# Five small edits to a fused attention and MLP kernel: sums, corner matmuls, staging, cosine, and which engine splits

## The chip, the cores and the metric

One core of one Trainium2 chip runs the whole program. The metric is the device time of one execution in microseconds (us). The engines of the core are named as in the profile: PE (TensorE matmuls), PEld (TensorE weight loads), DVE (VectorE), ACT (ScalarE), POOL (GpSimd), and SP, which here only issues DMAs.

## The reference, cut to what matters

The program is an attention with a learned bias, followed by two MLP layers. Everything is float32, the weights come as 8-byte floats.

```
scores = q @ k.T / 8 + bias(h, i, j)          # 4 batches x 8 heads, 576 x 576, head size 64
attn   = exp(scores - max) ; attn = attn / (sum(attn) + 1e-9)
x      = attn @ v                              # -> 2304 tokens x 512
h = x @ w_in1 ; x1  = (h * cos(h)) @ w_out1    # 512 -> 2048 -> 512
h = x1 @ w_in2; out = (max(h,0) + alpha*min(h,0)) @ w_out2
```

bias(h, i, j) is a small MLP of log1p(|i-j|) / log1p(max(i,1)) with 32 hidden values.

## The kernel before, in words

**Precision by splitting.** A float32 operand is cut into a rounded high part (`hi`) and the rest (`lo = x - hi`), and each product is three matmuls: hi*hi, hi*lo, lo*hi. The high part is a copy to a rounded type, the low part a subtraction. Five places do this: `split_qk` for q and k (high part of q on ACT in L312, of k on DVE in L314, both low parts on POOL in L319), `weight` for weights (L183 to L188), `split_x` for the MLP's inputs (L594 on DVE, L596 on DVE and POOL in turns), `split_g` for the activations (L641 on ACT, L642 on POOL).

**Bias.** 36 groups (`bias_phase`) of DVE, PE and ACT work write the bias matrix to memory; they fill the first 90 us or so and are interleaved with the first attention stages.

**Attention.** 16 pairs (two heads of one batch), each in two units: A (row blocks 0 and 1) and B (row blocks 2 and 3 and the remaining 64 rows of both heads, stage 0). The first four pairs do their A units first. A stage is `emit_S` (scores on PE, in 64-row tiles of the array; one PSUM buffer), `emit_max` (L348, DVE: adds the bias, takes the row maximum) and `emit_exp` (L360, ACT, with row sums). When all stages of a unit are through, `recip` adds 1e-9 to the sums (L368), inverts them (L369) and has POOL spread them over 64 columns (`rb`, L371). Then come the unit's fillers on PE, in the order that ORDER gives: 0 to 3 and R transposes (`T_full`, `T_rem`), v to z products with v (`PV`, L441 and L444), L the last transposes (`T_last`, L426 and L430), N the transposes of the inverse sums (`norm`, L379 and L384). They are put between the scores of the next stages by a credit of 1 us per half stage. In unit B, L and N each end with two matmuls of 64 x 64 corners (L430 and L384; each is four passes in the trace, since float32 takes two passes). L392 and L394 are the copies out of PSUM on ACT and DVE. Transposes take turns on three PSUM banks (`t_bank`).

**Staged weights.** The first eight of the 16 blocks of layer 1's weights are converted during attention and written to memory (`stage_w`, 16 pieces): load, L169 and L170 on ACT, L172 and L173 on DVE, L176 on POOL, high part on ACT (L184), low part on DVE (L188), store (L195). There is one buffer `st`. A new piece is let in at half stage WS0 + WSR * ns; `step` advances one generator by one yield per half stage, of the first two in the list in turns, and the rest runs after the last stage. The other eight blocks of layer 1 are converted directly during the first token tile of the MLP (`direct_w`).

**MLP.** Per layer 5 token tiles (3 of 512, 2 of 384 tokens) times 16 blocks f. `emit_h` (L608, 12 matmuls) fills one of four PSUM banks; `act1` applies h*cos(h): ACT writes h/(2 pi) + 1/4 (L617), DVE rounds it to a whole number by adding and subtracting a large constant (L618), takes that many turns off h in two steps (L619, L620), ACT takes the sine (L622), DVE multiplies by h (L623), which frees the bank; then L641 and L642. `emit_o` (L658, L660, 12 or 9 matmuls) follows four blocks behind; `evac` (L668, L670) empties its banks at the end of a tile.

**Order.** A planner with a model of durations puts the instructions of each engine in order; each engine then runs its list strictly in that order.

Of the kernel before, what the change touches and what calls it, by code (L numbers as in the profile page):

```python
# [19 lines left out]
B, H, S, D = 4, 8, 576, 64  # L20
# [4 lines left out]
NCC = DM // 128  # L25
HS = S // 2
NG = S // 16
MAGIC = 12582912.0
C1 = 6.28125
C2 = 2.0 * math.pi - C1  # L30
TILES = [(0, 512), (512, 512), (1024, 512), (1536, 384), (1920, 384)]
PITCH = S + 32
QC = S + 64
HP, LP, XP, CPRI, SP = 200, 0, 300, -50, 400
HIA = (1, 1, 1, 1)
LOP = (0, 0, 0, 0)
EV_A, EV_M = 5, 6
UPB, EPB = {"D": 11, "A": 4}, 4
PBUF, BTB = 6, 10
FIRST, SIDE, SMOD, BFIRST, BRATE, SPL, WS0, WSR, PER = 4, 6, 2, 16, 1.25, 3, 24, 7.3, 1.0  # L40
XL, XS, OEB, LA = 7, 12, 3, 4
KEEP = (1, 1)
QUOTA0, QUOTA1, NSF = 9, 2, 8
# [1 line left out]

UNIT = {"A": ((0, 1), 0), "B": ((2, 3), 1)}

ORDER = {"A": "012vw3LNxyz", "B": "01R2vw3LNxyz"}
TENG = {"A": "vava-a", "B": "vavava"}


# [6 lines left out]
def attn_mlp_kernel(ctx: ExitStack, tc: tile.TileContext, a: dict, out: bass.AP):  # L58
    nc = tc.nc
    ve, se, ge, te, sy = nc.vector, nc.scalar, nc.gpsimd, nc.tensor, nc.sync  # L60
# [99 lines left out]
    def weight(layer, f, part, hi, lo, hi_act, lo_pool):  # L160
        src = (a["wi1"], a["wi2"])[layer][f] if part == 0 else (a["wo1"], a["wo2"])[layer][f * 128:(f + 1) * 128, :]
        nm = f"{layer}_{f}_{part}"
        if wide:
            raw = wpool["s"].tile([128, 512, 2], I32, tag="raw", name=f"raw{nm}")
            sy.dma_start(out=raw.rearrange("p n t -> p (n t)"), in_=src.bitcast(I32))
            yield
            c = wpool["c"].tile([128, 512], I32, tag="c", name=f"wc{nm}")
            p = wpool["c"].tile([128, 512], I32, tag="p", name=f"wp{nm}")
            se.activation(out=c.bitcast(F32), in_=raw[:, :, 1].bitcast(F32), func=AF.Copy, scale=2.0 ** -112)  # L169
            se.activation(out=p, in_=raw[:, :, 0].bitcast(U32), func=AF.Copy, scale=2.0 ** -29)  # L170
            yield
            ve.tensor_scalar(c, c, 3, None, op0=ALU.logical_shift_left)  # L172
            ve.scalar_tensor_tensor(out=c, in0=raw[:, :, 1], scalar=-2 ** 31, in1=c,  # L173
                                    op0=ALU.bitwise_and, op1=ALU.bitwise_or)
            yield
            ge.tensor_tensor(out=c, in0=c, in1=p, op=ALU.add)  # L176
            yield
            w = c.bitcast(F32)
        else:
            w = wpool["s"].tile([128, 512], F32, tag="raw", name=f"raw{nm}")  # L180
            sy.dma_start(out=w, in_=src)
            yield
        if hi_act:  # L183
            keep(0, se.activation(out=hi, in_=w, func=AF.Copy))  # L184
        else:
            keep(0, ve.tensor_copy(out=hi, in_=w))
        yield
        keep(1, (ge if lo_pool else ve).tensor_tensor(out=lo, in0=w, in1=hi.bitcast(F32), op=ALU.subtract))  # L188
        yield
# [42 lines left out]
    def attention():  # L232
        with ExitStack() as c:
# [26 lines left out]
            Pp = {}  # L260
            Tt = {}
            T5t = {}
            xps = {}
            raws = {}
            sums = {}
            Rt = {}
            place = {(1 + i, h): (u, 2 * x + h) for u, (t, rem) in UNIT.items() for x, i in enumerate(t) for h in range(2)}
            place[0, 0] = ("B", 4)
            count = {"s": 0, "t": 0, "x": 0}

            def turn(which, pools):
                count[which] += 1
# [2 lines left out]
            def t_bank(name):  # L275
                return turn("t", ps_t).tile([128, 512], F32, tag="t", name=name)
# [29 lines left out]

            def split_qk(n):
                t = []
                for r, nm, eng in zip(raws.pop(n), "qk", (se, ve)):
                    hi, lo = (qk_p.tile([128, QC], F32R, tag=nm + x, name=f"{nm}{x}{n}") for x in "hl")  # L310
                    if eng is se:
                        se.activation(out=hi, in_=r, func=AF.Copy)  # L312
                    else:
                        ve.tensor_copy(out=hi, in_=r)  # L314
                    t.append((r, hi, lo))
                yield
                qk[n] = [x for r, hi, lo in t for x in (hi, lo)]
# [38 lines left out]
            def emit_exp(n, s, h, e, nm):  # L356
                u, col = place[s, h]
                if (n, u) not in sums:
                    sums[n, u] = m_p.tile([128, 5], F32, tag="sm", name=f"sm{n}_{u}")
                keep(3, se.activation(out=e, in_=e, func=AF.Exp, bias=nm, scale=-1.0,  # L360
                                      accum_out=sums[n, u][:, col:col + 1]))
                Pt[n, s, h] = e


            def recip(n, u):
                m = 4 + SIZE[u][1]
                sm = sums.pop((n, u))[:, 0:m]
                ve.tensor_scalar(sm, sm, 1e-9, None, op0=ALU.add)  # L368
                ve.reciprocal(out=sm, in_=sm)  # L369
                rb = x_p.tile([128, 5, 64], F32, tag="rb", name=f"rb{n}_{u}")  # L370
                ge.tensor_copy(out=rb[:, 0:m, :], in_=sm.unsqueeze(2).to_broadcast([128, m, 64]))  # L371
                Rt[n, u] = rb

            def norm(n, u):
                t, rem = SIZE[u]
                rb = Rt[n, u]
                ps = t_bank(f"N{n}_{u}")
                for x in range(t):
                    te.transpose(out=ps[:, 128 * x:128 * x + 128],  # L379
                                 in_=rb[:, 2 * x:2 * x + 2, :].rearrange("p a b -> p (a b)"), identity=ident)  # L380
                if rem:
                    for h in range(2):
                        r = slice(64 * h, 64 * h + 64)
                        te.matmul(ps[r, 128 * t:128 * t + 64], lhsT=rb[r, 4, :], rhs=ident[r, r],  # L384
                                  start=True, stop=True)
                R = x_p.tile([128, 320], F32, tag="R", name=f"R{n}_{u}")
                cpy("a", R[:, 0:QW[u]], ps[:, 0:QW[u]])
                Rt[n, u] = R
# [23 lines left out]
            def T_rem(n, u, eng):  # L412
# [4 lines left out]
                                 identity=ident)  # L417
                cpy(eng, Tt[n, u][:, :, :, w:w + 64], ps.rearrange("p (c h q) -> p c h q", c=4, h=2))

            def T_last(n, u, eng):  # L420
                t, rem = SIZE[u]
                T5 = T_p.tile([128, 320], F32, tag="T5", name=f"T5{n}_{u}")
                T5t[n, u] = T5
                ps = t_bank(f"T5{n}_{u}")
                for x, i in enumerate(UNIT[u][0]):
                    te.transpose(out=ps[:, 128 * x:128 * x + 128], in_=Pp[n, i][:, 512:640], identity=ident)  # L426
                if rem:
                    for h in range(2):
                        r = slice(64 * h, 64 * h + 64)
                        te.matmul(ps[r, 128 * t:128 * t + 64], lhsT=Pt[n, 0, 0][r, 512:S], rhs=ident[r, r],  # L430
                                  start=True, stop=True)
                cpy(eng, T5[:, 0:QW[u]], ps[:, 0:QW[u]])

            def PV(n, u, cc):
# [137 lines left out]
    def mlp():  # L572
        with ExitStack() as c:
# [38 lines left out]
            def act1(t, f, ps):  # L612
                n = TILES[t][1]
                h = ps[:, 0:n]
                tt = t_p.tile([128, 512], F32, tag="ta", name=f"ta{t}_{f}")[:, 0:n]
                g = t_p.tile([128, 512], F32, tag="tb", name=f"tb0_{t}_{f}")[:, 0:n]
                se.activation(out=tt, in_=h, func=AF.Identity, scale=1.0 / (2.0 * math.pi), bias=quart)  # L617
                ve.tensor_scalar(tt, tt, MAGIC, MAGIC, op0=ALU.add, op1=ALU.subtract)  # L618
                ve.scalar_tensor_tensor(out=g, in0=tt, scalar=-C1, in1=h, op0=ALU.mult, op1=ALU.add)  # L619
                ve.scalar_tensor_tensor(out=g, in0=tt, scalar=-C2, in1=g, op0=ALU.mult, op1=ALU.add)  # L620
                yield
                se.activation(out=g, in_=g, func=AF.Sin, bias=hpi)  # L622
                ve.tensor_tensor(out=g, in0=h, in1=g, op=ALU.mult)  # L623
                split_g(0, t, f, g)
                yield
# [165 lines left out]
```

## Time and profile before

| | us |
|---|---|
| median of 3 runs | 1198.11 (1197.49 to 1198.72) |
| profiled execution | 1197.57 |
| span of its instructions | 1195.7 |

Busy share of the span: PE 94%, PEld 74%, DVE 63%, ACT 45%, POOL 32%. PE's share is a sum over overlapping, pipelined matmuls; that it is high says that PE seldom stands still, not that its work could not be shorter. The attention fills the first 375 us or so, layer 1 of the MLP runs from there to about 800 us, layer 2 to the end.

### The profile page before, as it was taken

Reading aid. Unit: us, or ns where it says so; the run is one execution under the profiler, and the core shown is the slowest. Engines: PE = TensorE matmul, PEld = TensorE weight load, DVE = VectorE, ACT = ScalarE, POOL = GpSimd, SP = SyncE. Lnnn points to the kernel's source line nnn. Section 1 sums busy time; section 2 is a strip of 40 time slices with the busy share of each in tenths; the row PEclk is TensorE's granted clock in tenths of the full one; section 3 lists DMA queues with packets and bytes.
Section 4 is the critical chain, followed back from the end, with each engine's and each line's share of the span. In section 5 each row is a group of like instructions: output and inputs, shape, how many; then the busy total and the mean of one; then the engine's idle time right before and its main releaser. Section 6 shows DMA issues by size and latency. Waiting matters only on the chain.

```text
span 1195.7 us, 17301 instructions
## 1 busy us (share of the span) xinstructions
PE 1128.2 (94%) x6376; PEld 890.5 (74%) x6376; DVE 758.1 (63%) x1390; ACT 536.5 (45%) x1038; POOL 388.4 (32%) x330
## 2 busy tenths in 40 slices
PE   5688999899999898899999999999999999999998
PEld 1145666566666687688888999998788888899997
DVE  7897677877767899756756757787652242242322
ACT  5786676666763775443444554544411111111111
POOL 4003333333103555323333334354542222222222
PEclk7798999999999899899999999999999999999999
DMA  7764655656214544212112224644220010000000
GB/s 243 225 181 154 193 185 186 225 192 197 87 50 153 198 127 138 71 51 82 71 55 79 104 68 148 224 149 154 88 71 1 15 48 1 25 38 1 27 1 27
DMA packets 56084, 129.47 MB, mean 108 GB/s; under 512 B 8000, under 2 KB 15168, under 8 KB 53952
## 3 DMA queue, kind: packets, MB, share of 16 engines
q1 hardware_dynamic: 53696, 111.60, 28.7%
q0 software_dynamic: 2304, 16.78, 4.2%
q8 instruction: 50, 0.82, 0.3%
q14 instruction: 34, 0.28, 0.1%
HBM read 86.53 MB, written 41.83 MB: 107 GB/s over the span
## 4 chain that ended last, share of the span: by engine, by line
PE 53%; DVE 11%; DMA 6%; ACT 3%; issue 3%; POOL 1%; SPq 0%; DVEq 0%; ACTq 0%; POOLq 0%
PE h L608 23%; PE o L660 14%; PE o L658 10%; DMA raw<-in_wo_dram 3%; DVE tb L620 2%; PE S L332 2%; DVE wc L173 1%; DMA raw<-in_wi_dram 1%; DVE tb L619 1%; DVE w L188 1%; DVE tb L623 1%; DVE ta L618 1%; PE x_A L444 1%; PE x_B L444 1%; ACT tb L622 1%
## 5 line engine op out<-in xcount | busy, mean ns | idle before, releaser
L608 PE MATMUL h<-xhi,w 128*128 128x512 f32 (+1 forms) x1280 | 395.5, 371 | 8.0 <-DVE tb L623 4.9
L642 POOL TENSOR_TENSOR glo<-tb,ghi 128x512 fp32r<-128x512 f32 (+1 forms) x160 | 197.4, 1234 | 429.6 <-ACT ghi L641 404.9
L608 PEld LDWEIGHTS h<-xhi,w 128*128 128x128 f32 x1280 | 238.7, 189 | 42.9 <-DVE tb L623 5.3
L608 PE MATMUL h<-xlo,w 128*128 128x512 f32 (+1 forms) x640 | 237.1, 371 | 0.0
L641 ACT ACTIVATE ghi<-tb 128x512 fp32r<-128x512 f32 (+1 forms) x160 | 93.6, 586 | 316.8 <-PE o L660 254.1
L658 PE MATMUL o<-ghi,w 128*128 128x512 f32 (+1 forms) x640 | 199.1, 371 | 4.6 <-DVE oe L670 4.6
L660 PE MATMUL o<-w,ghi 128*128 128x512 f32 x576 | 192.0, 392 | 0.0
L631 DVE TENSOR_SCALAR tb<-h,alpha 128x512 f32<-128x512 f32 (+1 forms) x80 | 55.6, 695 | 198.7 <-PE h L608 187.8
L658 PEld LDWEIGHTS o<-ghi,w 128*128 128x128 f32 x640 | 119.7, 189 | 20.9 <-ACT ghi L641 5.0
L608 PEld LDWEIGHTS h<-xlo,w 128*128 128x128 f32 x640 | 120.8, 189 | 17.8 <-issue 0.5
L176 POOL TENSOR_TENSOR wc<-wc,wp 128x512 int32<-128x512 int32 x64 | 88.5, 1383 | 113.1 <-DVE wc L173 86.1
L660 PEld LDWEIGHTS o<-w,ghi 128*128 128x128 f32 x576 | 108.1, 188 | 22.4 <-issue 0.2
L658 PE MATMUL o<-glo,w 128*128 128x512 f32 (+1 forms) x320 | 118.8, 371 | 0.0
L660 PE MATMUL o<-w,glo 128*128 128x512 f32 x288 | 113.1, 393 | 1.0 <-POOL glo L642 1.0
L360 ACT ACTIVATE P<-P,nm 128x576 f32<-128x576 f32 x128 | 98.3, 770 | 33.1 <-DVE nm L348 33.0
L348 DVE CUSTOM_DVE_ANT_0 P<-S,bt 128x576 f32<-128x576 f32 x128 | 91.4, 749 | 16.4 <-PE S L332 6.9
L623 DVE TENSOR_TENSOR tb<-h,tb 128x512 f32<-128x512 f32 (+1 forms) x80 | 50.8, 635 | 62.7 <-ACT tb L622 62.3
L622 ACT ACTIVATE tb<-tb,hpi 128x512 f32<-128x512 f32 (+1 forms) x80 | 54.0, 674 | 73.3 <-DVE tb L620 73.1
L620 DVE SCALAR_TENSOR_TENSOR tb<-ta,tb 128x512 f32<-128x512 f32 (+1 forms) x80 | 74.8, 936 | 1.7
L170 ACT ACTIVATE wp<-raw 128x512 int32<-128x512 uint32 x64 | 42.8, 669 | 66.7 <-DMA raw<-in_wi_dram 36.5
L332 PE MATMUL S<-kh,qh 64*128 64x288 f32 (+1 forms) x288 | 56.7, 348 | 16.3 <-DVE nm L348 15.3
L658 PEld LDWEIGHTS o<-glo,w 128*128 128x128 f32 x320 | 60.5, 189 | 8.3 <-POOL glo L642 0.4
(98 smaller groups left out, 1612.3 us busy)
## 6 DMA issues: line engine op xcount, KB each, us to landing
raw<-in_wi_dram SPq DMA_DIRECT2D x32, 512.0 KB, 3.6
raw<-in_wo_dram SPq DMA_DIRECT2D x32, 512.0 KB, 3.6
w_d<-st SPq DMA_DIRECT2D x32, 512.0 KB, 3.3
w<-w_d POOLq DMA_DIRECT2D x16, 1024.0 KB, 7.2
bias_d<-be SPq DMA_DIRECT2D x36, 295.5 KB, 3.5
xlo<-x_d SPq DMA_DIRECT2D x24, 256.0 KB, 4.0
rq<-in_q_dram SPq DMA_DIRECT2D x16, 320.0 KB, 3.3
rk<-in_k_dram SPq DMA_DIRECT2D x16, 320.0 KB, 3.8
```

Of the source, the lines that this page charges most:

```text
L176: ge.tensor_tensor(out=c, in0=c, in1=p, op=ALU.add)
L332: te.matmul(ps[:, hf, 0:HS], lhsT=w[r, 128 * i:128 * i + 128], rhs=m[r, c0:c0 + HS], start=(j == 0), stop=(j == 2))
L348: keep(2, ve.tensor_tensor_reduce(out=sn.rearrange("p (a b) -> p a b", a=2), in0=ps[:, :, 0:HS], in1=bt[hp, s].rearrange("p (a b) -> p a b ...
L360: keep(3, se.activation(out=e, in_=e, func=AF.Exp, bias=nm, scale=-1.0, accum_out=sums[n, u][:, col:col + 1]))
L608: te.matmul(ps[:, 0:n], lhsT=w_[:, wx, w], rhs=xx[:, 0:n], start=(j == 0), stop=(j == 11))
L620: ve.scalar_tensor_tensor(out=g, in0=tt, scalar=-C2, in1=g, op0=ALU.mult, op1=ALU.add)
L622: se.activation(out=g, in_=g, func=AF.Sin, bias=hpi)
L623: ve.tensor_tensor(out=g, in0=h, in1=g, op=ALU.mult)
L641: se.activation(out=ghi[:, 0:n], in_=g, func=AF.Copy)
L642: ge.tensor_tensor(out=glo[:, 0:n], in0=g, in1=ghi[:, 0:n].bitcast(F32), op=ALU.subtract)
L658: te.matmul(acc[L, t][i][:, 0:n], lhsT=w_[:, wx, wl], rhs=gx[:, 0:n], start=st, stop=sp)
L660: te.matmul(acc[L, t][i], lhsT=gx[:, sl], rhs=w_[:, wx, 512:1024], start=st, stop=sp)
```

## The change

- `recip`: the sums of a unit live in one of six permanent tiles of 5 pairs (`sume`), whose second values are 1e-9 from the start; a DVE reduction over each pair replaces the addition of 1e-9.
- The two 64 x 64 corner matmuls of L and N use all 128 rows of their operand and the half of the identity that picks the rows (128 x 64 tiles). They are fillers of their own, M (`T_corner`) and O (`norm_last`), and stand ahead of 3, L and N in unit B.
- WSR is 6.5 in place of 7.3.
- `act1`: L617 writes int32, which rounds; L618 is gone. L619 and L620 read the int32 tile.
- `split_qk`: both high parts on POOL. HIA and LOP: the staged weights of layer 1 have their high and low parts on POOL. Directly converted weights and those of layer 2 are as before.

```diff
-HIA = (1, 1, 1, 1)
-LOP = (0, 0, 0, 0)
+HIA = (2, 1, 1, 1)
+LOP = (1, 0, 0, 0)
...
-FIRST, SIDE, SMOD, BFIRST, BRATE, SPL, WS0, WSR, PER = 4, 6, 2, 16, 1.25, 3, 24, 7.3, 1.0
+FIRST, SIDE, SMOD, BFIRST, BRATE, SPL, WS0, WSR, PER = 4, 6, 2, 16, 1.25, 3, 24, 6.5, 1.0
...
-ORDER = {"A": "012vw3LNxyz", "B": "01R2vw3LNxyz"}
+ORDER = {"A": "012vw3LNxyz", "B": "01R2vwMO3LNxyz"}
...
-        if hi_act:
+        if hi_act == 2:
+            keep(0, ge.tensor_copy(out=hi, in_=w))
+        elif hi_act:
             keep(0, se.activation(out=hi, in_=w, func=AF.Copy))
...
+            sume = [cp.tile([128, 5, 2], F32, tag=f"sume{i}", name=f"sume{i}") for i in range(6)]
+            for t in sume:
+                ge.memset(t, 1e-9)
...
-                for r, nm, eng in zip(raws.pop(n), "qk", (se, ve)):
+                for r, nm in zip(raws.pop(n), "qk"):
                     hi, lo = (qk_p.tile([128, QC], F32R, tag=nm + x, name=f"{nm}{x}{n}") for x in "hl")
-                    if eng is se:
-                        se.activation(out=hi, in_=r, func=AF.Copy)
-                    else:
-                        ve.tensor_copy(out=hi, in_=r)
+                    ge.tensor_copy(out=hi, in_=r)
...
-                    sums[n, u] = m_p.tile([128, 5], F32, tag="sm", name=f"sm{n}_{u}")
+                    count["m"] += 1
+                    sums[n, u] = sume[count["m"] % len(sume)]
                 keep(3, se.activation(out=e, in_=e, func=AF.Exp, bias=nm, scale=-1.0,
-                                      accum_out=sums[n, u][:, col:col + 1]))
+                                      accum_out=sums[n, u][:, col, 0:1]))
...
-                sm = sums.pop((n, u))[:, 0:m]
-                ve.tensor_scalar(sm, sm, 1e-9, None, op0=ALU.add)
+                sm = m_p.tile([128, 5], F32, tag="sm", name=f"sm{n}_{u}")[:, 0:m]
+                ve.tensor_reduce(out=sm, in_=sums.pop((n, u))[:, 0:m, :], op=ALU.add, axis=mybir.AxisListType.X)
                 ve.reciprocal(out=sm, in_=sm)
...
+            def corner(ps, w):
+                for h in range(2):
+                    te.matmul(ps[64 * h:64 * h + 64, 256:320], lhsT=w, rhs=ident[:, 64 * h:64 * h + 64],
+                              start=True, stop=True)
+
+            def norm_last(n, u):
+                Nt[n, u] = t_bank(f"N{n}_{u}")
+                corner(Nt[n, u], Rt[n, u][:, 4, :])
...
-                        te.matmul(ps[r, 128 * t:128 * t + 64], lhsT=rb[r, 4, :], rhs=ident[r, r],
-                                  start=True, stop=True)
...
+            def T_corner(n, u):
+                T5t[n, u] = t_bank(f"T5{n}_{u}")
+                corner(T5t[n, u], Pt[n, 0, 0][:, 512:S])
...
-                        te.matmul(ps[r, 128 * t:128 * t + 64], lhsT=Pt[n, 0, 0][r, 512:S], rhs=ident[r, r],
-                                  start=True, stop=True)
...
+                ops["M"] = (0.1, lambda: T_corner(n, u))
+                ops["O"] = (0.1, lambda: norm_last(n, u))
...
-                tt = t_p.tile([128, 512], F32, tag="ta", name=f"ta{t}_{f}")[:, 0:n]
+                tt = t_p.tile([128, 512], I32, tag="ta", name=f"ta{t}_{f}")[:, 0:n]
                 g = t_p.tile([128, 512], F32, tag="tb", name=f"tb0_{t}_{f}")[:, 0:n]
                 se.activation(out=tt, in_=h, func=AF.Identity, scale=1.0 / (2.0 * math.pi), bias=quart)
-                ve.tensor_scalar(tt, tt, MAGIC, MAGIC, op0=ALU.add, op1=ALU.subtract)
```

## Rows read from the trace of the kernel before

**Rows 1.** By stretch: length; busy (count) PE, PEld, DVE, ACT, POOL; clock, DMA, GB/s.
```profile
110.00:370.00 260.00, 242.58 (x1961) 162.24 (x1962) 192.30 (x459) 175.30 (x398) 69.74 (x67) 1.00 0.49 156
400.00:450.00 50.00, 50.00 (x221) 41.14 (x220) 48.58 (x68) 35.55 (x59) 28.65 (x21) 1.00 0.44 137
490.00:500.00 10.00, 5.36 (x15) 4.00 (x14) 7.89 (x11) 4.33 (x9) 3.96 (x3) 0.66 0.51 175
500.00:1190.00 690.00, 688.97 (x3281) 600.33 (x3281) 357.27 (x548) 211.76 (x365) 230.97 (x192) 1.00 0.20 66
```

**Rows 2.** Waits of PE from 385 to 520: who for whom, us, times, longest.
```profile
PE h L608 <- DVE tb L623: 4.9, 1, 4.9
PE o L658 <- DVE oe L670: 4.6, 1, 4.6
PE h L608 <- DVE w L188: 3.1, 2, 1.7
```

**Rows 3.** The chain that ended last: start us, us, what.
```profile
392.93 5.15 PE h L608 x12
...
464.78 2.79 PE h L608 x12
...
495.37 4.18 PE o L658 x9
```

**Rows 4.** ACT in order of time: start us, us, instruction, idle time before it and releaser.
```profile
382.49 0.67 ACT L169 ACTIVATE wc<-raw 128x512 f32<-128x512 f32 x1 [6.14 <-DVE st L188]
...
388.97 0.63 ACT L184 ACTIVATE st<-wc 128x512 fp32r<-128x512 f32 x1 [4.66 <-DMA w_d<-st]
```

**Rows 5.** Groups by line and shape: busy us, mean ns, idle before.
```profile
L170 ACT ACTIVATE wp<-raw 128x512 int32<-128x512 uint32 x64 | 42.8, 669 | 66.7 <-DMA raw<-in_wi_dram 36.5 <-DMA raw<-in_wo_dram 29.4 <-POOL glo L642 0.7
...
L618 DVE TENSOR_SCALAR ta<-ta 128x512 f32<-128x512 f32 x48 | 28.4, 593 | 21.0 <-ACT ta L617 21.0
```

**Rows 6.** Waits of PE from 110 to 370.
```profile
PE S L332 <- DVE nm L348: 9.8, 12, 1.3
PE x_B L444 <- ACT T_B L392: 3.1, 4, 2.2
PE T_B L407 <- DVE T_B L394: 1.9, 2, 1.4
```

**Rows 7.** PE in order of time, around the last transposes of a unit A and of a unit B.
```profile
213.39 0.44 PE L426 MATMUL T_A<-ident,P 128*128 128x128 f32 x2
213.67 0.38 PE L379 MATMUL N_A<-ident,rb_A 128*128 128x128 f32 x2
...
222.91 0.44 PE L426 MATMUL T_B<-ident,P 128*128 128x128 f32 x2
223.28 0.33 PE L430 MATMUL T_B<-ident,Pr 64*64 64x64 f32 x4
223.71 0.40 PE L332 MATMUL S<-kh,qh 64*128 64x288 f32 x2
```

**Rows 8.** POOL, DVE and PE in order of time, 216 to 222.
```profile
216.35 2.11 POOL L319 TENSOR_TENSOR ql<-rq,qh 128x640 fp32r<-128x640 f32 x1 [6.62 <-DMA bt<-bias_d]
...
216.95 1.86 DVE L314 CAST kh<-rk 128x640 fp32r<-128x640 f32 x1
...
221.30 0.46 POOL L371 COPY rb_B<-sm_B 128x320 f32<-128x320 f32 x1 [0.87 <-DVE sm_B L369]
...
221.10 0.66 PE L407 MATMUL T_B<-ident,P 128*128 128x128 f32 x4 [1.37 <-DVE T_B L394]
```

**Rows 9.** Single lines: duration ns min/median/max, first and last start, form.
```profile
L314 DVE CAST kh<-rk x16: 481/490/1857, 11.0 to 293.5; 128x640 fp32r<-128x640 f32 x16
...
L368 DVE TENSOR_SCALAR sm_B<-sm_B x16: 159/830/2626, 102.4 to 370.4; 128x5 f32<-128x5 f32 x16
...
L369 DVE RECIPROCAL sm_B<-sm_B x16: 173/186/192, 103.6 to 371.1; 128x5 f32<-128x5 f32 x16
...
L371 POOL COPY rb_B<-sm_B x16: 439/453/780, 111.7 to 371.5; 128x320 f32<-128x320 f32 x16
```

More of the change, by code (lines that the diff above doesn't have):

```diff
@@ L27 @@
 NG = S // 16
-MAGIC = 12582912.0
 C1 = 6.28125
@@ L262, in attention @@
             T5t = {}
+            Nt = {}
             xps = {}
@@ L268, in attention @@
             place[0, 0] = ("B", 4)
-            count = {"s": 0, "t": 0, "x": 0}
+            count = {"s": 0, "t": 0, "x": 0, "m": 0}
+            sume = [cp.tile([128, 5, 2], F32, tag=f"sume{i}", name=f"sume{i}") for i in range(6)]
+            for t in sume:
+                ge.memset(t, 1e-9)
             def turn(which, pools):
@@ L376, in norm @@
                 rb = Rt[n, u]
-                ps = t_bank(f"N{n}_{u}")
+                ps = Nt.pop((n, u)) if rem else t_bank(f"N{n}_{u}")
                 for x in range(t):
@@ L380, in norm @@
                                  in_=rb[:, 2 * x:2 * x + 2, :].rearrange("p a b -> p (a b)"), identity=ident)
-                if rem:
-                    for h in range(2):
-                        r = slice(64 * h, 64 * h + 64)
-                        te.matmul(ps[r, 128 * t:128 * t + 64], lhsT=rb[r, 4, :], rhs=ident[r, r],
-                                  start=True, stop=True)
                 R = x_p.tile([128, 320], F32, tag="R", name=f"R{n}_{u}")
@@ L418, in T_rem @@
                 cpy(eng, Tt[n, u][:, :, :, w:w + 64], ps.rearrange("p (c h q) -> p c h q", c=4, h=2))
+            def T_corner(n, u):
+                T5t[n, u] = t_bank(f"T5{n}_{u}")
+                corner(T5t[n, u], Pt[n, 0, 0][:, 512:S])
             def T_last(n, u, eng):
-                t, rem = SIZE[u]
                 T5 = T_p.tile([128, 320], F32, tag="T5", name=f"T5{n}_{u}")
+                ps = T5t.pop((n, u)) if SIZE[u][1] else t_bank(f"T5{n}_{u}")
                 T5t[n, u] = T5
-                ps = t_bank(f"T5{n}_{u}")
                 for x, i in enumerate(UNIT[u][0]):
                     te.transpose(out=ps[:, 128 * x:128 * x + 128], in_=Pp[n, i][:, 512:640], identity=ident)
-                if rem:
-                    for h in range(2):
-                        r = slice(64 * h, 64 * h + 64)
-                        te.matmul(ps[r, 128 * t:128 * t + 64], lhsT=Pt[n, 0, 0][r, 512:S], rhs=ident[r, r],
-                                  start=True, stop=True)
                 cpy(eng, T5[:, 0:QW[u]], ps[:, 0:QW[u]])
@@ L468, in fillers @@
                 ops.update({"vwxyz"[k]: (0.00167 * QW[u], lambda k=k: PV(n, u, k)) for k in range(5)})
-                ops["L"] = (0.11 * t + 0.1 * rem, lambda: T_last(n, u, e[4]))
-                ops["N"] = (0.11 * t + 0.1 * rem, lambda: norm(n, u))
+                ops["L"] = (0.11 * t, lambda: T_last(n, u, e[4]))
+                ops["N"] = (0.11 * t, lambda: norm(n, u))
+                ops["M"] = (0.1, lambda: T_corner(n, u))
+                ops["O"] = (0.1, lambda: norm_last(n, u))
                 ops["R"] = (0.44, lambda: T_rem(n, u, e[5]))
```

## The prediction

> **What bounds the kernel now.** I read the busy table by stretch first, then the waits of PE stage by stage, then the chain that ended last where those waits are long, and last the engine that stood there. From 500 us on PE is busy 688.97 of 690 us at full clock [rows 1]: 58% of the span that nothing but fewer or shorter matmuls can shorten, and the change removes none there. What it can win lies before.
>
> There are two places. The first is the first token tile of the MLP. PE waits there 4.9 us for a multiplication of DVE that frees a bank, 3.1 us in two waits for the low part of directly converted weights, 4.6 us for DVE's copy out of the accumulators [rows 2]; after the first and the last the matmuls are slow for a while: twelve took 5.15 us where they usually take 2.79, and nine took 4.18 [rows 3], and in 490 to 500 the granted clock is 0.66 on average, a mixture of its two levels, 1.2 and 2.4 GHz, after a wait in which PE did nothing [rows 1]. So 5.15 - 2.79 = 2.4 us and 4.18 - 9 x 2.79/12 = 2.1 us come on top; all together 17.1 us. DVE is the cause: it is busy 48.58 of the 50 us from 400 to 450 [rows 1], and the weights and activations that PE waits for are its work.
>
> The second is the attention. From 110 to 370 PE is busy 242.58 of 260 us [rows 1]. The idle 17.4 us are mostly waits for the row maximum on DVE (9.8), for ACT's copy of transposes (3.1) and DVE's (1.9) [rows 6]. DVE is 74% busy there and POOL 27%, so work moved from DVE and ACT to POOL goes to the emptier engine.
>
> **The change part by part.** *Rounding by int32* takes L618 away: 593 ns on average for 512 columns [rows 5], 80 instructions in all, but those after 500 us are free already, since PE does not wait there. In the first tile there are 16. A block takes PE 2 x 2.72, about 5.45 us, so 50 us hold 9.2 blocks, and DVE drops from 48.58 to 48.58 - 9.2 x 0.593 = 43.1 us, 86%. ACT's writing of int32 costs nothing: 669 ns for L170, which writes it [rows 5], against 0.67 us for the same shape in float [rows 4]. That L619 and L620 read an int32 operand is not to be seen in the trace; a gain is excluded, since the width is the same, and the loss is at most what L618 gave (0.6 us a block, which would leave DVE as it is). I take nothing. Then the 3.1 us go, since they are pure lack of DVE time, and of the third wait and its slow matmuls (6.7 us) I take the 4.6: DVE has about 16 x 0.59 = 9.5 us less to catch up with at the tile's end.
>
> *The first wait* (4.9 + 2.4 = 7.3 us) is a chain on ACT: it stood 6.14 us for a staged low part on DVE, later 4.66 us because a store had not left the only `st` buffer [rows 4]; the first sine stands behind that. With both parts of the staged pieces on POOL the second stand is POOL's. Queued behind it there is the low part of the first activation, which `emit_o` of block 0 needs. The sine could then come some 4.7 us earlier, and bank 0 is free before PE asks for it; but POOL still has to do the high and low part after the store, 0.7 + 1.7 us (453 ns x 512/320 for the copy; 2.11 us x 512/640 for the subtraction [rows 9, 8]), before it comes to the activation. I leave 2.3 us of the 7.3 for that and take 5.0. Bounds: nothing to 7.3. For the first tile that makes 5.0 + 3.1 + 4.6 = 12.7 us, with ends 0 and 17.1.
>
> *Sums over pairs.* L368 had a median of 830 ns and a maximum of 2626 for five columns; the reciprocal behind it, as small, never took over 192 [rows 9]. A reduction of ten values lies between 0.15 and 0.83; I take 0.19, the nearest row. *The high part of k* took 490 ns as a rule, but 1857 where POOL's low part of q, 2.11 us, ran beside it, and shortly after PE waited 1.37 us for DVE's copy of transposes [rows 8, 9]. So per pair DVE is rid of 0.7 (L314, between its short and its long ones, nearer the short), 0.83 - 0.19 = 0.64 (L368) and 0.54 (the staged low part, taken to be as long as ACT's 0.67 for that tile [rows 4], in 13 of 16 pairs), together 1.9 us, and ACT of about 1.2, on a pair's time of some 20 us. Which of PE's waits that removes is a matter of place: the 1.9 behind DVE's copy, most of the 3.1 behind ACT, little of the 9.8, since the maximum there stood behind a sum that waited for ACT's exponentials, and the reduction will wait for the same ones. Sum 5.0 us, ends 0 and 14.
>
> The Trainium skill (SBUF — State Buffer, Who interferes with whom) says that a DVE instruction in a 2-port mode or with two SBUF inputs and a GpSimd instruction exclude each other for a whole instruction, and that a reduction never takes part. The 1857 against 490 agree with the first, the reciprocal's 192 with the second at most by likeness. The rule speaks against the change too: by it the copies that POOL gets would block DVE as the subtractions did; what that would take is worked out in the second rival.
>
> *POOL's load.* Added per pair: two high parts of 640 columns, 2 x 0.9 us (453 ns x 640/320, an upper figure), and per staged piece 0.7 + 1.7. From 110 to 370 that is 12 x 1.8 + 13 x 2.4 = 53 us on top of 69.74 of 260 [rows 1], 47%: covered on average. The high parts are let in three stages, some 12 us, ahead of the scores that need them, so 5.7 us of splitting in a row (0.9 + 0.9 + 2.1 + 1.8) fit. If the cover is gone, `rb` is what is late, since POOL works strictly in order; that is the slower rival.
>
> *Corners.* Going from transposes into a 64 x 64 corner costs PE 223.28 - 222.91 = 0.37 us for the two transposes ahead, where two transposes followed by transposes take 0.28 [rows 7]: 0.09 for the change of tiles, twice a pair. Out of it I can read nothing certain: four passes and the way out take 0.43. Behind `w` the corners find the array already in 128 x 64 tiles and go through in one row; I take the two entries and 0.06 for the ways out, 0.24 a pair, 3.8 us in 16. Ends: 8 passes at the transposes' pace (0.14) are 1.12 against 2 x 0.52, a loss of 1.3 us; half of the 1.04 saved would be 8.3 us. Their two banks are held longer, but the number of banks taken per unit and their turns stay.
>
> *WSR* does nothing. A piece takes nine yields and one is run per half stage: 16 x 9 = 144 against the 120 half stages that are left after the 24th. The list is never empty, so letting pieces in earlier only makes it longer; the last three pieces end after the attention in either case. 0 us.
>
> *Before 110 us* four of the casts leave DVE, which was waiting in order for their loads, and four copies leave ACT; POOL's added 8 x 0.9 us run beside DVE's bias work and can block it. I take 2.0 us won, with ends of 6 won and 5 lost. The six small fills on POOL at the start lie in its idle time.
>
> **The sum** against the profiled execution (1197.57 us, the span 1195.7 and 1.9 around it): 12.7 + 5.0 + 3.8 + 2.0 = 23.5, so 1174.1; that execution lay 0.5 below the median of the runs, so 1174.6.
>
> **Rivals.**
> 1. *The attention keeps its length.* PE's own work is 93% of it, and a wait that goes may only come back at the next maximum. For it: 9.8 of the waits are of this kind. Against it: the 1.37 us behind the blocked cast. Then only the first tile heals: 1198.1 - 12.7 = 1185.
> 2. *The lock moves instead of going.* POOL's added 53 us block L172, L173 and the bias work as the low part of q blocked L314 (1.4 us more each time [rows 9]); 13 x 2 of them make 36 us, more than the 16 x 1.9 = 30 that DVE gains. The attention's 5.0 and 2.0 fall away; if the same holds in the first tile, where L620 stands beside POOL, its 7.7 behind DVE's load go too: 1174.6 + 14.7 = 1189. The lock is the Trainium skill's, from the section named.
> 3. *Slower: POOL is late with `rb`.* O stands right behind `w` now, while N came two fillers later. If in each of the 12 later pairs the two high parts (1.8) and a staged piece's (2.4) stand ahead of L371, `rb` comes 4.2 us later; about 1.1 of slack at `w` (its end at 222.91, `rb`'s at 221.30 + 0.46 [rows 7, 8]) leaves 3.1 a pair on PE, 37 us: 1174.6 + 37 = 1211. From 2.0 us a pair on (23.5 / 12) the kernel is slower than before. For it: POOL is strictly in order and also waits for loads and stores. Against it: the planner sees these durations and puts `rb` ahead if it can.
> 4. *All waits go*, those for the maximum too, and the corners halve: 17.1 + 14 + 8.3 = 39: 1159.
>
> **How the numbers follow.** Forecast 0.50, first rival 0.20, second 0.12, third 0.10, fourth 0.08. The range from 1162 to 1194 holds all but the third, most of the fourth and a little of the second. What a measurement of this kernel can tell from no change is 0.2%, 2.4 us. The third is slower (0.10, with 0.01 for a milder one), 0.03 of the second may come out as no change, and 0.86 is faster.
>
> **What would show it.** In the first tile: L618 absent, DVE under 90% from 400 to 450, none of the three waits of [rows 2] over 2 us, no stretch there with the clock below full. In the attention: L368's successor near 0.2 us, the MLP's first matmul some 10 us earlier, no PE wait for `rb` at O, POOL at 45 to 50%. The forecast is wrong if the MLP's first matmul does not move, if DVE stays at 97% without L618 (an int32 operand is slow), or if PE's waits name L371 or the high parts.

## The result, and the profile after

| | us | ratio to before, 95% interval |
|---|---|---|
| before, in the same comparison | 1198.41 (1197.49 to 1203.31) | |
| changed | 1188.24 (1187.04 to 1189.10) | 0.9909 [0.9887, 0.9930] |
| predicted | 1174.6 (1162.0 to 1194.0) | 0.9804 |

The change gives 0.9%, some 10 us of the 23.5 forecast; the interval lies below 1, and the time lies inside the range. The profiled execution of the changed kernel took 1189.1 us (span 1187.3).

Four moments split the two spans. Up to the start of the 145th score matmul (of 864) the changed kernel gains 1.3 us (110.5 to 109.2); from there to the 841st it takes 247.1 us in place of 250.8; from there to the MLP's first matmul 12.4 in place of 12.8; and from there to the end 818.7 in place of 821.6. So the attention gave 3.7 + 0.4 where 8.8 were forecast (5.0 from its waits, 3.8 from the corners), and the MLP 2.9 where 12.7 were.

The stretches of [rows 1] after; same columns. The last is 10 us shorter, since the span is.

```profile
110.00:370.00 260.00, 249.42 (x1981) 164.47 (x1981) 169.74 (x441) 161.38 (x373) 108.89 (x121) 0.99 0.49 160
400.00:450.00 50.00, 48.65 (x214) 39.66 (x212) 47.56 (x59) 34.51 (x59) 29.14 (x20) 1.00 0.36 116
490.00:500.00 10.00, 10.00 (x40) 8.04 (x39) 4.15 (x7) 4.07 (x7) 2.58 (x2) 0.89 0.17 64
500.00:1180.00 680.00, 679.22 (x3239) 592.27 (x3239) 329.79 (x481) 206.05 (x357) 228.49 (x190) 1.00 0.20 66
```

In the attention the edits did on the engines what they say: DVE from 192.3 to 169.7 us, ACT from 175.3 to 161.4, POOL from 69.7 to 108.9. In the first tile DVE, without L618, is still busy 47.56 of 50 us.

PE's waits after, from 385 to 520 (answering to [rows 2]) and from 110 to 370 (to [rows 6]).

```profile
PE o L667 <- ACT oe L677: 4.1, 1, 4.1
PE o L667 <- ACT ghi L650: 2.5, 1, 2.5
PE h L618 <- DVE w L189: 2.5, 2, 1.4
```

```profile
PE x_B L452 <- ACT T_B L402: 5.2, 3, 2.3
PE S L335 <- DVE nm L351: 4.6, 12, 0.5
PE T_B L417 <- DVE T_B L404: 0.7, 2, 0.4
```

The three waits of the first tile are all still there under other names: 4.1 for 4.6 at the tile's end, 2.5 for 4.9 at its start, 2.5 for 3.1 between. In the attention the wait for the maximum is halved, and the one for ACT's copies has grown.

Where matmuls are missing, by windows of 10 us (PE, PEld, DVE, ACT, POOL, clock; a full window holds some 45.5):

```profile
380.00:390.00 10.00, 7.49 (x26) 5.60 (x26) 8.29 (x13) 7.36 (x11) 6.46 (x7) 0.83 0.86 307
440.00:450.00 10.00, 8.65 (x38) 6.69 (x37) 9.93 (x11) 6.39 (x11) 5.91 (x5) 1.00 0.45 154
450.00:460.00 10.00, 8.86 (x39) 7.05 (x38) 9.60 (x14) 6.77 (x11) 6.00 (x4) 1.00 0.37 120
480.00:490.00 10.00, 5.94 (x18) 4.49 (x18) 7.19 (x11) 5.83 (x10) 4.23 (x3) 0.77 0.47 147
```

With 490 to 500 above (40 matmuls) the start of the tile loses 19.5 matmuls, its middle 14, its end 33, that is 4.3, 3.1 and 7.3 us at 4.55 matmuls a us. Before it was 7.7 (35 and 21 in 380 to 400), 3.6 (29 in 450 to 460) and 6.7. Only the start has got better.

### The profile page after: what moved, and what is told of

Its sections match the earlier page's. It is cut to its first block, busy times and chain, and to the rows that moved or that the text cites. A ratio compares the mean times of both kernels' runs of the same rounds, so it can differ in the third digit from the quotient of the medians.

```text
span 1187.3 us, 17185 instructions
## 1 busy us (share of the span) xinstructions
PE 1131.0 (95%) x6376; PEld 890.8 (75%) x6376; DVE 699.5 (59%) x1278; ACT 516.6 (44%) x1006; POOL 439.1 (37%) x400
## 4 chain that ended last, share of the span: by engine, by line
PE 72%; DVE 11%; DMA 7%; ACT 4%; issue 3%; POOL 1%; SPq 0%; DVEq 0%; ACTq 0%; POOLq 0%
PE h L618 25%; PE o L669 14%; PE o L667 13%; PE S L335 5%; DMA raw<-in_wo_dram 4%; PE x_B L452 3%; PE x_A L452 2%; PE T_B L417 2%; DVE P L351 2%; PE bps L123 2%; PE T_A L417 1%; DVE u L118 1%; DMA raw<-in_wi_dram 1%; DVE wc L172 1%; DVE w L189 1%
## 5 line engine op out<-in xcount | busy, mean ns | idle before, releaser
L618 PE MATMUL h<-xhi,w 128*128 128x512 f32 (+1 forms) x1280 | 394.7, 370 | 2.5 <-DVE w L189 2.5
L618 PEld LDWEIGHTS h<-xhi,w 128*128 128x128 f32 x1280 | 238.4, 188 | 37.5 <-DVE w L189 3.3
L618 PE MATMUL h<-xlo,w 128*128 128x512 f32 (+1 forms) x640 | 237.2, 371 | 0.0
L667 PEld LDWEIGHTS o<-ghi,w 128*128 128x128 f32 x640 | 120.1, 190 | 23.5 <-ACT oe L677 4.5
L618 PEld LDWEIGHTS h<-xlo,w 128*128 128x128 f32 x640 | 120.6, 188 | 17.9 <-POOL xlo L606 0.5
L628 DVE SCALAR_TENSOR_TENSOR tb<-ta,h 128x512 f32<-128x512 int32 (+1 forms) x80 | 50.4, 629 | 62.0 <-ACT ta L627 42.0
```

What stands on the lines that cost most here:

```text
L618: te.matmul(ps[:, 0:n], lhsT=w_[:, wx, w], rhs=xx[:, 0:n], start=(j == 0), stop=(j == 11))
L667: te.matmul(acc[L, t][i][:, 0:n], lhsT=w_[:, wx, wl], rhs=gx[:, 0:n], start=st, stop=sp)
```

## The experiments

Each ratio is to runs of the kernel before on the same chip; "alone" means the kernel before with this part of the change only.

**One part at a time.** e1: int32, L618 gone. e2: high parts of q and k on POOL. e3: staged parts on POOL. e4: corners (M, O, 128 x 64). e5: sums over pairs. e6: WSR.

```diff
e1  tt = ...I32, and the line of L618 gone
e2  -if eng is se: se.activation(out=hi, ...) else: ve.tensor_copy(out=hi, in_=r)   +ge.tensor_copy(out=hi, in_=r)
e3  -HIA = (1, 1, 1, 1); LOP = (0, 0, 0, 0)   +HIA = (2, 1, 1, 1); LOP = (1, 0, 0, 0)
e4  +corner(), T_corner, norm_last; ORDER["B"] = "01R2vwMO3LNxyz"
e5  +sume, tensor_reduce   -tensor_scalar(+ 1e-9)
e6  -WSR 7.3   +WSR 6.5
```

> The kernel before with the int32 rounding alone (L618 gone). Forecast's theory (lack of DVE time in the first token tile): 3.1 + 4.6 = 7.7 us faster, 1190.7, DVE well under 90% from 400 to 450. Rival, the ring: a block's multiplication, high part and low part hold one of two `tb` buffers, and blocks wait in turn for POOL's low part, so DVE is blocked or waiting for as long as L618 took; then at most 2 us faster, 1196.5 to 1198.4, and the waits of PE at the end of the first tile stay.

> The kernel before with the high parts of q and k on POOL alone. If the blocked casts of k on DVE were what PE waited for in the attention: 3 to 4 us faster, 1194.5 to 1195.5, the wait for DVE's copies of transposes gone. If PE's own work sets the attention: within 1.5 us of before.

> The kernel before with both parts of the staged weights on POOL alone. Forecast's theory: the first wait of the first tile (ACT standing behind a store) falls from 4.9 to some 2 us, and DVE and ACT are freer in the attention: 5 to 7 us faster, 1191.5 to 1193.5. Rival (the stand moves to POOL with its full length, the attention is PE's own work): within 2 us of before.

> The kernel before with the corners as M and O in 128 x 64 tiles alone. Forecast: 3.8 us faster, 1194.6. If a change of tiles costs PE nothing that shows: no difference. If PE waits for `rb` at O: slower, with PE waits that name L371 ahead of the corner.

> The kernel before with the sums over pairs alone. If L368's blocked 0.83 us held up DVE's copies and maxima: 1 to 3 us faster, 1195.5 to 1197.5. If PE's own work sets the attention: no difference.

> The kernel before with WSR 6.5 alone. By the count of steps only the first three pieces move by a half stage or two: no difference in cause. What differs shows how much a new order by the planner alone can move the time; expected within 2 us of before.

| alone | median us | ratio | 145th to 841st score | MLP from |
|---|---|---|---|---|
| before (profiled) | | | 250.8 | 374.1 |
| e1 int32 | 1198.74 | 0.9993 [0.9967, 1.0019] | 250.1 | 371.2 |
| e2 q, k on POOL | 1194.78 | 0.9957 [0.9939, 0.9976] | 247.8 | 369.7 |
| e3 staged on POOL | 1192.65 | 0.9944 [0.9924, 0.9964] | 247.0 | 370.3 |
| e4 corners | 1203.19 | 1.0037 [1.0017, 1.0056] | 257.1 | 380.3 |
| e5 sums | 1198.58 | 0.9989 [0.9968, 1.0009] | 254.0 | 377.3 |
| e6 WSR | 1202.99 | 1.0024 [1.0001, 1.0048] | 256.8 | 380.6 |

(The two columns on the right are from one profiled execution each, the median is over all runs.) Both moves to POOL gain, as much as was expected of them. The rounding, of which the prediction expected the most, gains nothing alone that can be told, nor do the sums; the interval of the rounding leaves room for 4 us, not for the 7.7. The corners lose 4.4 us without any PE wait for `rb`, and WSR 2.9, clear of zero by little; neither loss was expected.

**The first tile.** A block takes PE some 5.45 us, so the pace of the activations matters where they are behind, above all at the tile's end. Theory: with two `tb` buffers a ring sets that pace, and POOL's low part is in it; L618 was in the shadow of that ring. e7 puts L618 back into the changed kernel; e8 adds a third `tb` buffer to the changed kernel (the turns in int16, to make room); e10 does so with int32 turns and one `oe` buffer less; e11 is e10 with L618 back.

```diff
e7   +ve.tensor_scalar(tt, tt, MAGIC, MAGIC, op0=ALU.add, op1=ALU.subtract)   (tt in F32)
e8   -tt = ...I32, tag="ta"   +tt = ...int16, tag="ta"    -tag="tb"   +tag="tb", bufs=3
e10  -tag="tb"   +tag="tb", bufs=3                        -OEB = 3    +OEB = 2
e11  e10 with the line of e7
```

> The changed kernel with L618 back (float tile, rounding by the large constant). Forecast's theory: 7.7 us slower than the changed kernel, 1196. Ring: 0 to 2 us slower, 1188 to 1190.

> The changed kernel with three `tb` buffers in place of two (the turns are int16 to make room). Ring theory: the next block's first step no longer waits for POOL's low part of the block before; the wait of 4.1 us at the end of the first tile and its slow matmuls shrink, 4 to 7 us faster than the changed kernel, 1181 to 1184. If DVE's and ACT's load with weights is what holds the tile up, no difference, 1188.

> The changed kernel with three buffers for tb and two (not three) for oe; the turns stay int32. If the ring over the two tb buffers is what held the end of the first tile, and the width of the turns does not matter, the time is that of three buffers with int16 turns, 1181.3, or up to 3 us more for the missing oe buffer. If int16 was what helped there, it is the changed kernel's 1188.

> The same with three tb and two oe buffers, but with the rounding on DVE back (L618, float turns). With two tb buffers L618 cost nothing (1188.8 against 1188.2). Ring theory: with the ring open the blocks at the end of a tile follow each other in one chain of turns, rounding, two steps, sine, product; 0.6 us more a block for some 4 to 8 blocks, so 2 to 6 us slower than the run without L618. Rival: DVE has slack there in any case, and L618 costs nothing again (within 1 us).

| | two `tb` buffers, three `oe` | three `tb`, two `oe` |
|---|---|---|
| L618 there | e7: 1188.84, 0.9897 [0.9872, 0.9921]; MLP 819.0 | e11: 1192.02, 0.9944 [0.9921, 0.9967]; MLP 822.4 |
| L618 gone | changed: 1188.24; MLP 818.7 | e10: 1181.09, 0.9853 [0.9827, 0.9878]; MLP 811.5 |

("MLP" is from its first matmul to the end of the span.) e8 gives the same as e10: 1181.26, 0.9841 [0.9817, 0.9865], so it is the buffer and not the width of the turns. Removing L618 is worth 0.3 us in the MLP with two buffers and 10.9 with three (2 to 6 were expected). While L618 is there the third buffer gains nothing: e11 takes 3.2 us more than e7. (e11 also has one `oe` buffer less. That costs nothing without L618, as e8 and e10 show; with L618 it was not run by itself.) Each hides the other. The rows show how. DVE at the end of the tile, start us, us, instruction, idle before it; first of the changed kernel, then of e8:

```profile
475.30 0.69 DVE L628 SCALAR_TENSOR_TENSOR tb<-ta,h 128x512 f32<-128x512 int32 x1 [1.25 <-POOL glo L651]
476.02 0.69 DVE L629 SCALAR_TENSOR_TENSOR tb<-ta,tb 128x512 f32<-128x512 int32 x1
477.57 0.69 DVE L632 TENSOR_TENSOR tb<-h,tb 128x512 f32<-128x512 f32 x1 [0.85 <-ACT tb L631]
479.51 0.69 DVE L628 SCALAR_TENSOR_TENSOR tb<-ta,h 128x512 f32<-128x512 int32 x1 [1.25 <-POOL glo L651]
```

```profile
470.31 0.69 DVE L628 SCALAR_TENSOR_TENSOR tb<-ta,h 128x512 f32<-128x512 int16 x1 [0.47 <-ACT ta L627]
471.03 0.69 DVE L629 SCALAR_TENSOR_TENSOR tb<-ta,tb 128x512 f32<-128x512 int16 x1
472.57 0.69 DVE L632 TENSOR_TENSOR tb<-h,tb 128x512 f32<-128x512 f32 x1 [0.85 <-ACT tb L631]
473.73 0.69 DVE L628 SCALAR_TENSOR_TENSOR tb<-ta,h 128x512 f32<-128x512 int16 x1 [0.47 <-ACT ta L627]
```

A block takes 4.21 us in the one, 3.42 in the other. ACT and POOL of the changed kernel close the ring:

```profile
476.81 0.72 ACT L631 ACTIVATE tb<-tb,hpi 128x512 f32<-128x512 f32 x1 [2.38 <-DVE tb L629]
477.44 0.62 ACT L650 ACTIVATE ghi<-tb 128x512 fp32r<-128x512 f32 x1
```

```profile
478.19 1.29 POOL L651 TENSOR_TENSOR glo<-tb,ghi 128x512 fp32r<-128x512 f32 x1 [2.92 <-ACT ghi L650]
```

The high part at 477.44 belongs to the product that was ready at 473.36 + 0.69, but on ACT it stands behind the next block's sine. Its low part on POOL (478.19 to 479.48) frees the `tb` buffer for which L628 waits at 479.51; L628, L629 and the sine follow: sine, high part, low part, L628, L629 make 4.2 us. In the kernel before the same place looked otherwise, with nearly the same period (DVE, and below it POOL):

```profile
481.27 0.69 DVE L619 SCALAR_TENSOR_TENSOR tb<-ta,h 128x512 f32<-128x512 f32 x1
481.99 1.55 DVE L620 SCALAR_TENSOR_TENSOR tb<-ta,tb 128x512 f32<-128x512 f32 x1
484.39 0.69 DVE L623 TENSOR_TENSOR tb<-h,tb 128x512 f32<-128x512 f32 x1 [0.85 <-ACT tb L622]
485.00 0.41 DVE L618 TENSOR_SCALAR ta<-ta 128x512 f32<-128x512 f32 x1
485.52 0.69 DVE L619 SCALAR_TENSOR_TENSOR tb<-ta,h 128x512 f32<-128x512 f32 x1
...
481.70 1.30 POOL L642 TENSOR_TENSOR glo<-tb,ghi 128x512 fp32r<-128x512 f32 x1 [2.96 <-ACT ghi L641]
```

There the second step falls into POOL's low part (the last row), where it takes 1.55 us and not 0.69; product, rounding, two steps and sine follow each other in one chain of 4.25 us a block, and DVE shows no wait for a buffer. e11 does this again in spite of its third buffer:

```profile
474.93 0.69 DVE L630 SCALAR_TENSOR_TENSOR tb<-ta,h 128x512 f32<-128x512 f32 x1
475.65 1.55 DVE L631 SCALAR_TENSOR_TENSOR tb<-ta,tb 128x512 f32<-128x512 f32 x1
...
479.18 0.69 DVE L630 SCALAR_TENSOR_TENSOR tb<-ta,h 128x512 f32<-128x512 f32 x1
```

So the theory holds only for the kernel without L618. With L618 the chain with its blocked step sets the pace, at 4.25 us, whatever the buffers; without it the ring over two buffers does, at 4.21, and the time of L618 becomes a wait for a buffer. Only where both go do the blocks come faster.

**The corners.** e9: the changed kernel with the corners of before. e13: with the new shape, but in the old place.

```diff
e9   -M, O, corner(), norm_last, T_corner      +te.matmul(ps[r, ...], lhsT=rb[r, 4, :], rhs=ident[r, r]) in L and N
e13  -ORDER["B"] = "01R2vwMO3LNxyz"   +ORDER["B"] = "01R2vw3LNxyz"   (corner(ps, ...) called at the end of L and N)
```

> The changed kernel with the corner matmuls of the kernel before (64 x 64, at the end of L and N); all else as changed. If the corners themselves cost what they cost alone (4.4 us in the experiment that made only them), about 1184. If that loss was the order that the planner found around them, since PE's busy time from 110 to 370 did not grow there, it stays between 1186 and 1191. If they gain the 3.8 us of the prediction, 1192.

> The changed kernel with its 128 x 64 corner matmuls, but at the end of L and N, where the kernel before had the 64 x 64 ones; the order of the fillers is that of before. If what costs is the place (M and O ahead of 3 bring 301 changes of tile shape between the 13th and the 79th stage where the kernel without them has 256), the changes fall to about 256 and the time to that of the run with the old corners, 1180.2, within 2 us. If it is the shape of the corners, the time stays at 1188.

| | median us | ratio | 145th to 841st score | changes of tile shape there | idle PE there |
|---|---|---|---|---|---|
| before | | | 250.8 | 269 | 16.9 |
| e4, corners alone | 1203.19 | 1.0037 | 257.1 | 296 | 19.1 |
| changed | 1188.24 | 0.9909 [0.9887, 0.9930] | 247.1 | 297 | 9.8 |
| e9, without them | 1180.24 | 0.9836 [0.9806, 0.9866] | 240.2 | 252 | 9.4 |
| e13, new shape, old place | 1179.58 | 0.9826 [0.9798, 0.9855] | 239.6 | 244 | 9.2 |

(The changes are counted from PE's rows in order of time: a matmul whose tile, 128*128, 128*64, 64*128 or 64*64, is not that of the one before it.) It is the place, not the shape: e13 has the new shape and the time of e9, and e9 came out below all that was expected of it (1184 to 1192). It holds beyond single executions: the six kernels with M and O beside the moves to POOL (changed, e7, e8, e10, e11, e12) took 245.9 to 250.6 us there, the four without them (e9, e13, e14, e15) 239.2 to 242.1. Waits and clock are not what differs: changed and e9 stand idle nearly equally long (9.8 and 9.4), and the granted clock from 112 to 350 us is 0.99 in changed, e9 and e13. The changed kernel has 45 changes more and takes 6.9 us more, 0.15 us for each if all of it is theirs, which no run shows by itself. Why there are more is seen in the order. Two corners (L382) of the changed kernel, and a unit B of e9, PE in order of time:

```profile
120.60 1.30 PE L452 MATMUL x_B<-T_B,v 128*64 128x320 f32 x8
121.72 0.28 PE L382 MATMUL N_B<-ident,rb_B 128*64 128x64 f32 x4
121.94 0.44 PE L394 MATMUL N_B<-ident,rb_B 128*128 128x128 f32 x2
122.31 1.30 PE L452 MATMUL x_B<-T_B,v 128*64 128x320 f32 x8
123.54 0.81 PE L449 MATMUL x_B<-T_B,v 128*128 128x320 f32 x2
124.27 0.34 PE L382 MATMUL N_B<-ident,rb_B 128*64 128x64 f32 x4
124.54 0.44 PE L394 MATMUL N_B<-ident,rb_B 128*128 128x128 f32 x2
```

```profile
216.35 1.30 PE L447 MATMUL x_B<-T_B,v 128*64 128x320 f32 x8
217.58 0.44 PE L429 MATMUL T_B<-ident,P 128*128 128x128 f32 x2
217.94 0.33 PE L433 MATMUL T_B<-ident,Pr 64*64 64x64 f32 x4
218.21 0.40 PE L334 MATMUL S<-kh,qh 64*128 64x288 f32 x2
```

The corner at 121.72 stands right behind products in 128*64 tiles and enters without a change, as the prediction had it; the one at 124.27 has a way into 128*64 tiles and one out. Of the 30 corners between the 145th and the 841st score matmul 10 are of the first kind and 20 of the second. That makes 40 changes that would not be there without them, where the corners of e9 make 35; the other 40 of the 45 are those of other fillers. From 110 to 362 us eight products go in a row to the transposes behind them 35 times in e9 and 3 times in the changed kernel, four in a row 15 and 33 times. So beyond their own entries M and O shifted the other fillers against each other. Alone (e4) 27 changes more and 2.2 us more idle time go with 6.3 us more; what is not idle time is again 0.15 us a change.

**The third wait, and all together.** e12 is e8 with the staging of layer 2's weights let in at other blocks; e14 is e12 with the corners of before; e15 is e14 with WSR 7.3.

```diff
-if L == 0 and 1 <= t <= 3 and f % 3 == 0 and ns < 16:
+if L == 0 and 1 <= t <= 4 and f % 3 == 2 and ns < 16:
```

> The changed kernel with three tb buffers, int16 turns, and the staging of layer 2's weights let in at blocks 2, 5, 8, 11, 14 of tiles 1 to 4 (before: blocks 0, 3, ... of tiles 1 to 3). If the piece that is let in at the first block of tile 1 holds up the copies out of the accumulators (1.9 us wait for ACT's copy, and the slow matmuls after it, with three buffers), both shrink: 1177 to 1180. Rival: PE waits there for the last activations all the same, 1180 to 1182.

> The changed kernel with the corners of before, three tb buffers, int16 turns, and the staging of layer 2's weights let in at blocks 2, 5, ... of tiles 1 to 4. If the gains lie in different stretches and add: 1188.2 - 8.0 (corners) - 11.6 (first tile) = 1168.6, first MLP matmul near 362.7 and no wait over 2.5 us from there on. If the first tile's waits come back when it starts earlier (the staged pieces are less far), 1172 to 1177.

> The run before it with WSR 7.3 as in the kernel before. If the 2.9 us that 6.5 alone cost are the staging's own, 2 to 5 us faster than with 6.5. If that loss was the order of that one program, no difference beyond 2 us in either direction that can be told ahead.

e12: 1176.58 us, 0.9814 [0.9786, 0.9841]; the MLP takes 808.0 in place of 811.5, and of PE's waits from 367 to 520 one is left:

```profile
PE o L667 <- ACT ghi L650: 2.5, 1, 2.5
```

So half of what the tile's end lost was the staged piece that stood between the last activations and the copies out of the accumulators. On ACT of the changed kernel it is this row ahead of the copy:

```profile
484.24 0.66 ACT L168 ACTIVATE wc<-raw 128x512 f32<-128x512 f32 x1 [1.46 <-DVE st L189]
...
485.37 0.59 ACT L677 ACTIVATE oe<-o 128x512 f32<-128x512 f32 x1
```

e14: 1173.97, 0.9768 [0.9732, 0.9803], the fastest beside e15: 1173.99, 0.9774 [0.9744, 0.9805]. Both beat the changed kernel (0.9909) and the one before. e14 is 5 us over the 1168.6 of gains that add. It lies where it was expected if the first tile's waits came back, but they did not (no wait of PE from 365 to 520 is over 1.4 us). In its profiled execution the 145th score began at 112.7 us and not at e9's 109.6, and the MLP took 809.4 us and not 818.7 - 11.6 = 807.1: PE waits 2.7 us for ACT's copy out of the accumulators at 790 us, a wait that e12 does not have. WSR, which lost 2.9 us alone, makes no difference here; the loss alone was a matter of the order that the planner found, or of something that these runs do not show.

## Why the prediction was wrong

**The step that failed first: "DVE is the cause".** The prediction took DVE's 97% [rows 1] as the limit of the first tile and let L618's 0.593 us a block come straight off: 86% instead of 97%, "the 3.1 us go, since they are pure lack of DVE time", and 4.6 of the third wait, 7.7 us in all. DVE went to 95%, and e1 and e7 put the worth of L618 near 0 (0.9993; 1188.84 against 1188.24). What stood in its place are two limits of nearly one length: with L618 the chain in which L620 is blocked beside POOL's low part, 4.25 us a block, and without it the ring over two `tb` buffers through ACT's order and POOL's low part, 4.21; with both open it is 3.42.

The first could have been read beforehand: L619 to L619 was 4.25 us in the trace of before with L620 at more than twice its undisturbed length, and POOL's low part there each time. The profile shows an engine as busy while it is blocked, so a part of the 97% was waiting. In before the 27 L620s of 512 columns with no POOL instruction beside them took 677 to 694 ns, the 21 beside one up to 1787, half of them over 1.7 us; L619, which reads one operand from PSUM, never took over 690 either way. L618 itself averaged 0.86 us from 395 to 475, where the prediction took 0.593 and it takes 0.41 to 0.43 alone. After the change it is the same: the means of L171, L172 and L629 are 0.76, 0.82 and 1.02 us there, alone mostly 0.42, 0.69 and 0.69. The Trainium skill (SBUF — State Buffer, Who interferes with whom) has a rule for it, an exclusive lock over the ports that DVE shares with GpSimd, which a DVE instruction with two SBUF inputs meets and one with at most one, outside the 2-port modes, does not; L620's 1.55 us beside POOL's subtraction against 0.69 alone, and L619's 0.69 in both cases, agree.

The prediction used that rule only for the edits that move work to POOL, and not for reading DVE's load. With the third buffer L618's time does count: 10.9 us between e11 and e10, more than the 9.5 us that were worked out for 16 blocks.

**The corners: the wrong sign.** Forecast 3.8 us won with ends of -1.3 and 8.3; measured 6.9 us lost (changed against e9), below the lower end. The step was "behind `w` the corners find the array already in 128 x 64 tiles and go through in one row". It holds for 10 of 30 corners; the other 20 stand between matmuls in 128*128 tiles. And the passes and entries were counted for the corner alone; what the two new fillers do to the order of the products and transposes around them was not. That M and O were taken as fixed at their place behind `w`, with all else as before, is what failed; in the old place the new shape costs nothing (e13 against e9).

**The attention's waits: the mechanism right in part, the size too small.** 5.0 us forecast; without the corners the stretch gets 10.6 shorter (250.8 to e9's 240.2). Of these, 7.5 are idle time (16.9 to 9.4): the relief of DVE and ACT works as argued, but of the 9.8 for the maximum, of which the prediction hoped for little, more than half went (4.6 are left in the changed kernel). The other 3.1 are no waits: PE's matmuls themselves take less, in an order with 17 changes of tile shape fewer (252 for 269). The prediction had PE's own work as fixed. That the sums alone bring nothing (e5) fits the reservation that the reduction waits for the same exponentials. e2 and e3 show 3.0 and 3.8 of it in their profiled executions.

**The first wait**: forecast 5.0 of 7.3; the loss at the tile's start fell from 7.7 to 4.3, so 3.4. As foretold, ACT stands no longer for a store. Its first stand, 6.14 us for the low part of `st` [rows 4], is 1.22 us for the same low part on POOL. The 2.3 us that were left for POOL did not come about: the first low part of the activations does not wait behind a staged piece there but for ACT's high part (the last row). What is left is the first block's chain on ACT, with that stand and a table load of 1.28 us in it.

```profile
380.75 0.67 ACT L168 ACTIVATE wc<-raw 128x512 f32<-128x512 f32 x1 [1.22 <-POOL st L189]
...
382.54 1.28 ACT L631 ACT_TABLE_LOAD   x1
...
385.31 0.63 ACT L650 ACTIVATE ghi<-tb 128x512 fp32r<-128x512 f32 x1 [0.19 <-DVE tb L632]
...
386.02 1.59 POOL L651 TENSOR_TENSOR glo<-tb,ghi 128x512 fp32r<-128x512 f32 x1 [1.85 <-ACT ghi L650]
```

**The third wait** was to lose 4.6 of 6.7 and became 7.3. That came half from the ring (e8: 1.9 left of 4.1) and half from the staged piece (e12).

**Right**: int32 costs nothing (L628 took 682 ns for 512 columns, as L619 in float did before), before 110 us 1.3 won for 2.0, and WSR at 0 within the whole. POOL was 42% busy where 47 was foretold. The sums' reduction, taken as 0.19, takes 0.15:

```profile
L372 DVE TENSOR_REDUCE sm_A<-sume x16: 146/160/164, 58.3 to 356.2; 128x4 f32<-128x8 f32 x16
L372 DVE TENSOR_REDUCE sm_B<-sume x16: 148/154/165, 104.8 to 365.4; 128x5 f32<-128x10 f32 x16
```

**The rivals.** The measured time lies between the first (1185) and the second (1189), but for neither's reason: the attention without corners did get shorter, and POOL's copies did not block DVE there by the 36 us of the second (its busy time fell by 22.6 us). That it came between them is luck: two misses of opposite sign, more won in the attention and as much lost by the corners. The third did not come: no wait of PE names `rb`. That a removed instruction turns into a wait of the same length, with POOL's low part at its end, was not among them.

In sum, of the 23.5: MLP -2.9 for -12.7, attention without the corners -10.6 for -5.0, corners +6.5 for -3.8 (6.9, less 0.4 on the way to the first MLP matmul), before 110 us -1.3 for -2.0: -8.3, the difference of the two spans to 0.1; the medians lie 10.2 apart.

## What to carry to other kernels

Before an instruction is counted as won because its engine is nearly full, follow one whole turn of the loop at that place and read which buffer closes it: the time per turn, not the busy share, says what a removal is worth, and a removal and a further buffer may be worth nothing singly and, as here, over 7 us together. Ask also what closes the turn once the first limit is gone. Busy time of DVE beside POOL contains waiting. A small operation on PE is priced with what its place does to the order of its neighbours, not by its own passes alone; change shape and place in separate steps.

## What the runs showed of the hardware

A wait of PE of some 2 us can cost nearly as much again behind it. In the changed kernel ACT stood for a load of weights, the copy of transposes behind it came late, PE waited 2.27 us, and the granted clock from 255 to 260 us was 0.67, a mixture of 1.2 and 2.4 GHz. ACT, then PE:

```profile
254.41 0.66 ACT L169 ACTIVATE wp<-raw 128x512 int32<-128x512 uint32 x1 [3.01 <-DMA raw<-in_wo_dram]
254.98 0.58 ACT L402 ACTIVATE T_B<-Tr 128x512 f32<-128x512 f32 x1
```

```profile
255.61 1.42 PE L452 MATMUL x_B<-T_B,v 128*64 128x320 f32 x8 [2.27 <-ACT T_B L402]
256.96 0.61 PE L335 MATMUL S<-kh,qh 64*128 64x288 f32 x2
257.37 0.44 PE L335 MATMUL S<-kl,qh 64*128 64x288 f32 x2
```

The pairs of score matmuls follow each other there at 0.24 us, elsewhere at 0.13. That pair of heads took 22.0 us, the median of the pairs 18.3. It is not so after each such wait: in the kernel before one of 2.2 us [rows 6] left the clock from 110 to 370 us at 1.00 [rows 1]. In e7, which differs in the MLP alone, two other pairs took 22.9 and 22.3 us and this one 19.4. So the attention of one program can differ by some us from one execution to the next, and e5's and e6's 3 and 6 us more in single profiles are not evidence of a cost: their granted clock from 110 to 370 us is 0.99 and 0.98, which by estimate is 2.6 and 5.2 us.

POOL's plain copies of 640 columns took 0.72 us (median), below the 0.9 that was scaled from the copy of 320, and its two-input operations on them 1.55 from 110 to 370 us, where the subtraction for q had a median of 1.88 in before and took 2.11 in the case shown.
